# Gated linear attention feeding two MLP stages: a reordered opening, and squared terms kept in PSUM

## The chip, the cores and the metric

The kernel runs on one core of a Trainium2 chip. The metric is the device time of one execution in microseconds. Engines are named as the profile names them: PE (TensorE matmul), PEld (its weight load), DVE (VectorE), ACT (ScalarE), POOL (GpSimd) and SP (SyncE, which issues DMAs here). PSUM is the memory that PE writes; it has eight banks of 512 float32 per partition. SBUF holds everything else on the chip.

## The reference, cut to what matters

```python
# q, k, v, alpha: (4, 8, 768, 48)
for t in range(S):
    state = alpha[:, :, t, :, None] * state + einsum('bhd,bhe->bhde', k[:, :, t], v[:, :, t])
    y[:, :, t] = einsum('bhd,bhde->bhe', q[:, :, t], state)
x = y.transpose(0, 2, 1, 3).reshape(3072, 384)
p = domain_probs / domain_probs.sum(-1)             # (3072, 4)
x = sum(p[:, e:e+1] * (relu(x @ w1[e]) @ w2[e]) for e in range(4))   # 384 -> 1024 -> 384
h = x @ w_in                                        # 384 -> 2048
out = (h - tanh(h)) @ w_out                         # 2048 -> 384
```

## The kernel before

**Attention.** The sequence is cut into chunks of 128 steps, so there are 24 *units* (6 chunks of 4 batches), each with all 8 heads. For a unit `st_scan` (line 246) makes the decay products: a forward scan (250) into the first half of `fg`, a maximum and a reciprocal on four columns (255, 256), a small product `fc` (259) that carries the decay to the batch's next chunk, and a backward scan (261) into the second half. `st_prod` (265) multiplies q and k by them, `st_scores` (282) forms scores on PE, `st_kt` copies transposed keys, `st_mask` (301) masks scores, `st_out` (311) makes the output on PE, `st_upd` and `st_state` carry the state, `st_y` (353) copies the output to SBUF and `st_store` (359) sends it to DRAM. `st_flag` (271) takes a range check on ACT. `a_load`, `qk_load` and `v_load` bring a unit's inputs.

**MLP stages.** These run as *steps* `(g, block, f)`: g 0 to 3 are the four experts (8 steps a block), g 4 is the last MLP (16 steps a block). Tokens go in blocks of 512; g 0 begins with two blocks of 256. Every float32 operand is split in two parts, high and low, so a step has nine matmuls in `mm1` (line 479, into one PSUM tile `ph`) and nine in `mm2` (line 523, into three tiles `po`). Between them `evac1` (494) makes `hh` on ACT and `hl` on DVE; for g 4, `evac2` (503) calls `h_minus_tanh` (64): four ACT passes (`gu`, `gt` and two squares, both named `gs` in the trace), a mask `gmk` on POOL and five DVE passes (lines 71 to 75); `evac2_out` (514) then splits the result, `hh` on ACT and `hl` on POOL. `mm2` runs one to three steps behind `mm1` (`flush(depth)`), two in most of g 4.

Weights are split in `w_prep` (396): a cast on ACT (407) and a subtraction on POOL (408). The weights of g 4 come as 64-bit words and are converted during g 1 to 3.

**Order.** It is written by hand: the program order of each engine's instructions is the order of the calls (`manual_schedule`), and each engine runs its own queue in order. During g 0 the attention's stages are strung between the steps by `points` (372), four points to a unit and about two steps to a unit. Before the steps stands an opening (lines 562 to 656): loads, the first two units, the first 256 tokens' split (`x_parts`, 459), the normalisation of the probabilities (`p_norm`, 596), the splits of the first eight weights, and dummy matmuls (`busy`, 577). `at.tile(..., bufs=n)` gives n rotating buffers to a tag; a new use of a buffer waits for the last reader of its old contents.

Of the kernel before, what the change touches and what calls it, by code (L numbers as in the profile page):

```python
# [8 lines left out]
F32 = mybir.dt.float32  # L9
# [5 lines left out]
ALU = mybir.AluOpType  # L15
# [3 lines left out]
P = 128  # L19
# [18 lines left out]
def f32(ap):  # L38
    return ap.bitcast(F32)
# [138 lines left out]
def tile_kernel(ctx: ExitStack, tc: tile.TileContext, qka, a0, v, vT, pT, w12, w64, out):  # L178
# [43 lines left out]

    def a_load(u):
        c, b = divmod(u, B)
        t = at.tile([112, 513], F32, name="aa", tag="aa", bufs=2)
        nc.sync.dma_start(out=t, in_=qka[c, b, :, 1024:1537])
        unit[u]["aa"] = t

    def qk_load(u):
        c, b = divmod(u, B)  # L230
        t = at.tile([112, 1024], F32, name="qk", tag="qk", bufs=2)
        nc.sync.dma_start(out=t, in_=qka[c, b, :, 0:1024])
        unit[u]["qk"] = t

    def v_load(u):
        c, b = divmod(u, B)
        vt = at.tile([P, DM], F32, name="vraw", tag="vraw", bufs=4)
        nc.sync.dma_start(out=vt, in_=v[c, b])
        unit[u]["vt"] = vt
# [3 lines left out]
            return pso.tile(shape, F32, name=f"po{i}", tag=f"po{i}")  # L243
        return psa.tile(shape, F32, name="pa", tag="pa")

    def st_scan(u):
        s = unit[u]
        fg = at.tile([112, 1024], F32, name="fg", tag="fg", bufs=2)
        c_, r_ = fg[:, 0:512], fg[:, 512:1024]
        nc.vector.tensor_tensor_scan(out=c_, data0=s["aa"][:, 0:512], data1=c_beg, initial=0.0,  # L250
                                     op0=ALU.mult, op1=ALU.add)
        c127 = c_.rearrange("p (j t) -> p j t", t=C)[:, :, C - 1]

        den = at.tile([112, 4], F32, name="den", tag="den")
        nc.vector.tensor_scalar(out=den, in0=c127, scalar1=2.0 ** -62, scalar2=None, op0=ALU.max)
        nc.vector.reciprocal(out=r_end.rearrange("p (j t) -> p j t", t=C)[:, :, C - 1], in_=den)
        if u < NU - B:
            fc = at.tile([112, 4], F32, name="fc", tag="fc", bufs=4)
            nc.vector.tensor_tensor(out=fc, in0=c127, in1=a0s[:, u + B], op=ALU.mult)
            s["fc"] = fc  # L260
        nc.vector.tensor_tensor_scan(out=r_[:, ::-1], data0=s["aa"][:, 1:513][:, ::-1], data1=r_end[:, ::-1],  # L261
                                     initial=0.0, op0=ALU.mult, op1=ALU.add)
        s["fg"] = fg

    def st_prod(u):
        s = unit[u]
        prod = at.tile([112, 1024], F32, name="prod", tag="prod", bufs=3)
        nc.vector.tensor_tensor(out=prod, in0=s["qk"], in1=s["fg"], op=ALU.mult)  # L268
        s["prod"] = prod

    def st_flag(u):
        s = unit[u]
        ab = at.tile([112, 1024], BF16, name="ab", tag="ab")
        nc.scalar.activation(ab, s["fg"], AF.Abs, accum_out=flags[:, u:u + 1])

# [77 lines left out]
    def st_y(u):  # L353
        s = unit[u]
        s["y"] = at.tile([112, 512], F32, name="y", tag="y", bufs=2)
        for hf, r in halves():
            nc.scalar.copy(s["y"][r], s["py"][r])

    def st_store(u):
        s = unit[u]  # L360
        for hf, r in halves():
            nc.sync.dma_start(
                out=xr[u // 2].rearrange("(j r) t -> r j t", r=2 * D)[hf * D:(hf + 1) * D, :, (u % 2) * C:(u % 2 + 1) * C],
                in_=s["y"][r].rearrange("e (j t) -> e j t", t=C))

# [93 lines left out]
    def x_parts(t0, n, kb):  # L459
        t, raw = xt[0, t0], xraw[t0]  # L460
        nc.scalar.copy(t[:, 0, kb, :n], raw[:, kb, :n])
        nc.vector.tensor_tensor(out=t[:, 1, kb, :n], in0=raw[:, kb, :n], in1=f32(t[:, 0, kb, :n]), op=ALU.subtract)  # L462
        if kb == KB - 1:
            o = t0 % 512
            nc.sync.dma_start(out=xs[t0 // 512][:, :, :, o:o + n], in_=f32(t[:, :, :, :n]))

    def p_load(g, t0, n):
        t = sp.tile([P, 512], F32, name="pb", tag="pb")
# [10 lines left out]
    def mm1(st):  # L479
        g, bi, t0, n, f, _ = st  # L480
        w, x = slot[g * 8 + f], xt[g, t0]
        r = len(phs) % 5
        phs.append(0)
        if g == 4 and r >= 2:
            ph = late["p"].tile([P, 512], F32, name="ph", tag=f"po{r - 2}")
        else:
            ph = psh.tile([P, 512], F32, name="ph", tag="ph")
        seq = [(a, b, kb) for a, b in ((0, 0), (1, 0), (0, 1)) for kb in range(KB)]
        for m, (a, b, kb) in enumerate(seq):
            nc.tensor.matmul(ph[:, :n], w[:, a, 0, kb * P:(kb + 1) * P], x[:, b, kb, :n],  # L490
                             start=m == 0, stop=m == len(seq) - 1)
        return ph
# [10 lines left out]
    def evac2(st, ph):  # L503
        gp = late["g"]
        gg = h_minus_tanh(nc, ph, ca, gp.tile([P, 512], F32, name="gg", tag="gg"),
                          sp.tile([P, 512], F32, name="gu", tag="pb"),
                          gp.tile([P, 512], F32, name="gt", tag="gt"),
                          sp.tile([P, 768], F32, name="gs1", tag="wraw")[:, :512],
                          gp.tile([P, 512], F32, name="gs2", tag="gs2"),
                          gp.tile([P, 512], F32, name="ghu", tag="ghu"),  # L510
                          gp.tile([P, 512], I32, name="gmk", tag="gmk"))
        ggs[st] = gg
# [48 lines left out]
    with tc.manual_schedule():  # L561
        a_load(0)
        qk_load(0)
        a_load(1)
        v_load(0)
        nc.sync.dma_start(out=a0s, in_=a0)
        qk_load(1)
        v_load(1)
        pr = at.tile([P, NE, 24], F32, name="pr", tag="pr")
        nc.sync.dma_start(out=pr, in_=pT.rearrange("e (p j) -> p e j", p=P))  # L570
        w_load(0)
        w_load(1)

        wu = at.tile([P, 512], BF16, name="wu", tag="wu")
        nc.gpsimd.memset(wu, 0.0)
# [29 lines left out]
                                    op=ALU.mult)  # L605
            nc.sync.dma_start(out=pn.rearrange("e (p j) -> p e j", p=P), in_=pr)

        st_scan(0)
        st_prod(0)
        st_load(0)  # L610
        st_scores(0)
        st_kt(0)
        st_scan(1)
        st_mask(0)
        st_prod(1)
        w_load(2)
        w_load(3)
        st_out(0)
        st_scores(1)
        st_kt(1)  # L620
        st_load(1)
        st_y(0)
        st_store(0)
        st_flag(0)
        w_prep(0)
        st_mask(1)
        st_upd(0)
        busy(4)
        st_out(1)
        st_y(1)  # L630
        st_store(1)
        x_load(0, 0, 256)
        st_upd(1)
        st_state(0)
        st_state(1)
        st_flag(1)
        w_prep(1)
        busy(8)
        points(3)
        w_load(4)  # L640
        w_load(5)
        w_load(6)
        w_load(7)
        for kb in range(KB):
            x_parts(0, 256, kb)
        points(4)
        p_norm()
        w_prep(2)
        w_prep(3)
        w_load(8)  # L650
        w_load(9)
        p_load(0, 0, 256)
        w_prep(4)
        w_prep(5)
        w_prep(6)
        w_prep(7)

        conv = [(i, hf) for i in range(16) for hf in range(2)]

# [7 lines left out]
        for si, st in enumerate(steps):  # L667
# [141 lines left out]
```

## Time and profile before

| what | value |
|---|---|
| time, median of 3 runs | 1368.82 us (1367.76 to 1369.43) |
| profiled execution: time, span | 1368.58 us, 1366.7 us |
| busy: PE, PEld, DVE, ACT, POOL | 97%, 77%, 62%, 39%, 38% |
| chain that ended last: PE, DVE, issue | 73%, 21%, 3% |
| DMA | 118.60 MB, mean 87 GB/s |

The span runs from the first to the last instruction of the profiled execution. Busy shares are means over stages that differ: up to about 280 us attention and the first expert run together, from there to 922 us the other experts, and from there to the end the last MLP. A matmul's recorded end is modelled, so the distance between starts tells more than busy time.

### The profile page before, as it was taken

Reading aid. Unit: us, or ns where it says so; the run is one execution under the profiler, and the core shown is the slowest. Engines: PE = TensorE matmul, PEld = TensorE weight load, DVE = VectorE, ACT = ScalarE, POOL = GpSimd, SP = SyncE. Lnnn points to the kernel's source line nnn. Section 1 sums busy time; section 2 is a strip of 40 time slices with the busy share of each in tenths; the row PEclk is TensorE's granted clock in tenths of the full one; section 3 lists DMA queues with packets and bytes.
Section 4 is the critical chain, followed back from the end, with each engine's and each line's share of the span. In section 5 each row is a group of like instructions: output and inputs, shape, how many; then the busy total and the mean of one; then the engine's idle time right before and its main releaser. Section 6 shows DMA issues by size and latency. Waiting matters only on the chain.

```text
span 1366.7 us, 17887 instructions
## 1 busy us (share of the span) xinstructions
PE 1321.5 (97%) x6850; PEld 1057.5 (77%) x6850; DVE 847.8 (62%) x1213; ACT 527.9 (39%) x918; POOL 516.3 (38%) x403
## 2 busy tenths in 40 slices
PE   6699999999999999999999999998999999999996
PEld 4588888888888888888888888886777777777774
DVE  7777666622344344333345443328999999999996
ACT  4234323323111123111122111116666767676664
POOL 5211011004111125111133111127887877777774
PEclk8799999999999999999999999999999999999999
DMA  8456544343322224223334323241000000000000
GB/s 260 111 154 201 152 121 142 121 135 117 118 86 80 86 77 170 78 78 100 100 123 146 101 100 100 78 139 47 1 24 1 24 1 24 0 24 0 24 1 27
DMA packets 51457, 118.60 MB, mean 87 GB/s; under 512 B 5792, under 2 KB 28576, under 8 KB 48416
## 3 DMA queue, kind: packets, MB, share of 16 engines
q1 hardware_dynamic: 51360, 117.35, 26.8%
q8 instruction: 56, 0.92, 0.3%
q14 instruction: 41, 0.34, 0.1%
HBM read 92.12 MB, written 25.21 MB: 86 GB/s over the span
## 4 chain that ended last, share of the span: by engine, by line
PE 73%; DVE 21%; issue 3%; ACT 1%; DMA 1%; DVEq 0%; SPq 0%; ACTq 0%
PE po L536 34%; PE ph L490 33%; DVE ghu L73 6%; DVE gg L74 4%; DVE gg L75 3%; DVE ghu L71 2%; PE pa L292 2%; PE pa L325 1%; PE pa L328 1%; PE pa L317 1%; PE pa L287 1%; DVE am L306 1%; DVE prod L268 1%; DVE fg L250 1%; DVE fg L261 0%
## 5 line engine op out<-in xcount | busy, mean ns | idle before, releaser
L490 PE MATMUL ph<-xt,w 128*128 128x512 f32 (+1 forms) x2664 | 643.2, 386 | 0.4 <-DVE xt L462 0.4
L490 PEld LDWEIGHTS ph<-xt,w 128*128 128x128 f32 x2664 | 493.7, 189 | 104.1 <-issue 1.0
L536 PE MATMUL po<-hh,w 128*128 128x512 f32 (+1 forms) x1776 | 458.9, 393 | 15.6 <-ACT hh L518 8.1
L499 DVE SCALAR_TENSOR_TENSOR hl<-ph,hh 128x512 fp32r<-128x512 f32 (+1 forms) x200 | 133.8, 669 | 445.5 <-ACT hh L498 445.0
L536 PEld LDWEIGHTS po<-hh,w 128*128 128x128 f32 x1776 | 321.4, 188 | 112.4 <-ACT hh L518 34.2
L498 ACT ACTIVATE hh<-ph 128x512 fp32r<-128x512 f32 (+1 forms) x200 | 116.2, 581 | 594.0 <-PE ph L490 555.6
L536 PE MATMUL po<-hl,w 128*128 128x512 f32 (+1 forms) x888 | 247.9, 387 | 4.0 <-DVE hl L499 2.4
L536 PEld LDWEIGHTS po<-hl,w 128*128 128x128 f32 x888 | 160.1, 188 | 46.1 <-POOL hl L520 10.5
L70 POOL TENSOR_SCALAR gmk<-gu 128x512 int32<-128x512 f32 x96 | 176.0, 1833 | 25.6 <-ACT gu L66 25.2
L520 POOL TENSOR_TENSOR hl<-gg,hh 128x512 fp32r<-128x512 f32 x94 | 121.6, 1294 | 91.1 <-ACT hh L518 91.1
L73 DVE SCALAR_TENSOR_TENSOR ghu<-gs,ghu 128x512 f32<-128x512 f32 x96 | 132.3, 1379 | 0.0
L74 DVE SCALAR_TENSOR_TENSOR gg<-gs,ghu 128x512 f32<-128x512 f32 x96 | 97.4, 1015 | 12.7
L518 ACT CAST hh<-gg 128x512 fp32r<-128x512 f32 x96 | 59.7, 621 | 106.5 <-DVE gg L75 106.5
L552 POOL TENSOR_TENSOR acc<-acc,ptmp 128x512 f32<-128x512 f32 x51 | 64.6, 1298 | 83.7 <-DVE ptmp L548 83.7
L408 POOL TENSOR_TENSOR w<-wraw,w 128x768 fp32r<-128x768 f32 x26 | 48.7, 1872 | 122.8 <-issue 66.4
L349 POOL TENSOR_TENSOR state<-state,fc 112x192 f32<-112x192 f32 x20 | 11.9, 597 | 181.6 <-DVE state L340 145.1
L432 POOL TENSOR_TENSOR w<-wf,w 128x384 fp32r<-128x384 f32 x16 | 16.3, 1016 | 164.8 <-ACT w L431 164.8
L75 DVE COPY_PREDICATED gg<-gmk,ph 128x512 f32<-128x512 int32 x96 | 72.0, 750 | 9.9
L432 POOL TENSOR_TENSOR wo<-wf,wo 128x384 fp32r<-128x384 f32 x16 | 16.2, 1015 | 155.0 <-ACT wo L431 155.0
L66 ACT ACTIVATE gu<-ph 128x512 f32<-128x512 f32 x96 | 57.6, 600 | 34.8 <-PE ph L490 23.2
L68 ACT ACTIVATE gs<-gu,ca 128x512 f32<-128x512 f32 x96 | 69.7, 726 | 0.0
L69 ACT ACTIVATE gs<-gu,ca 128x512 f32<-128x512 f32 x96 | 69.4, 723 | 0.0
(91 smaller groups left out, 945.0 us busy)
## 6 DMA issues: line engine op xcount, KB each, us to landing
xt<-xs SPq DMA_DIRECT2D x18, 1536.0 KB, 7.1
r<-w SPq DMA_DIRECT2D x32, 384.0 KB, 4.2
qk<-qka SPq DMA_DIRECT2D x24, 448.0 KB, 4.5
wraw<-w SPq DMA_DIRECT2D x26, 384.0 KB, 3.1
xs<-xt SPq DMA_DIRECT2D x5, 1536.0 KB, 6.0
w64s<-wo SPq DMA_DIRECT2D x16, 384.0 KB, 3.0
w<-w64s SPq DMA_DIRECT2D x8, 768.0 KB, 4.3
pb<-pn SPq DMA_DIRECT2D x23, 256.0 KB, 4.3
```

The costliest lines, as they stand in the source:

```text
L68: nc.scalar.activation(s1, u, AF.Square, bias=ca[:, 0:1])
L69: nc.scalar.activation(s2, u, AF.Square, bias=ca[:, 1:2])
L70: nc.gpsimd.tensor_scalar(out=mk, in0=u, scalar1=T2, scalar2=None, op0=ALU.is_gt)
L73: nc.vector.scalar_tensor_tensor(out=hu, in0=s1, scalar=B1, in1=hu, op0=ALU.add, op1=ALU.mult)
L74: nc.vector.scalar_tensor_tensor(out=gg, in0=s2, scalar=B2, in1=hu, op0=ALU.add, op1=ALU.mult)
L75: nc.vector.copy_predicated(out=gg, mask=mk, data=ph)
L490: nc.tensor.matmul(ph[:, :n], w[:, a, 0, kb * P:(kb + 1) * P], x[:, b, kb, :n], start=m == 0, stop=m == len(seq) - 1)
L498: nc.scalar.activation(a[:, :n], ph[:, :n], AF.Relu)
L499: nc.vector.scalar_tensor_tensor(out=b[:, :n], in0=ph[:, :n], scalar=0.0, in1=f32(a[:, :n]), op0=ALU.max, op1=ALU.subtract)
L520: eng.tensor_tensor(out=b, in0=gg, in1=f32(a), op=ALU.subtract)
L536: nc.tensor.matmul(po[d][:, :n], w[:, wi, 1, d * P:(d + 1) * P], r[:, :n], start=f == 0 and pi == 0, stop=f == (7 if g < 4 else 15) and pi ...
L552: nc.gpsimd.tensor_tensor(out=a_, in0=a_, in1=tmp, op=ALU.add)
```

## The change

The input loads of four units and the first weights are put ahead, with three buffers for `aa` and `qk` in place of two. `st_scan` is cut in two (`st_c`, `st_r`); the second unit's forward scan stands ahead of the first unit's mask and its backward scan behind it. The `fc` product moves into `st_flag`. Stores of the attention's output are issued by ACT in place of SP; half of the output copy of units 0 and 1 goes to DVE. Weight splits 2 and 3 stand between the first points, and 4 to 7 behind steps 0 to 3; `p_norm` and the loads of weights 8 and 9 behind step 4. The store of the split x goes behind step 3 of its block (`x_keep`). In g 4 the tile `ph` has three places in turn in place of five, and the two banks set free hold `gs1` and `gs2`, one buffer each; before, these were in SBUF with two each.

```diff
-        t = at.tile([112, 513], F32, name="aa", tag="aa", bufs=2)
+        t = at.tile([112, 513], F32, name="aa", tag="aa", bufs=3)
-        t = at.tile([112, 1024], F32, name="qk", tag="qk", bufs=2)
+        t = at.tile([112, 1024], F32, name="qk", tag="qk", bufs=3)
...
     def st_flag(u):
         s = unit[u]
+        if u < NU - B:
+            s["fc"] = at.tile([112, 4], F32, name="fc", tag="fc", bufs=4)
+            nc.vector.tensor_tensor(out=s["fc"], in0=s["fg"].rearrange("p (j t) -> p j t", t=C)[:, 0:4, C - 1],
+                                    in1=a0s[:, u + B], op=ALU.mult)
...
         for hf, r in halves():
-            nc.scalar.copy(s["y"][r], s["py"][r])
+            if u < 2 and hf:
+                nc.vector.tensor_copy(s["y"][r], s["py"][r])
+            else:
+                nc.scalar.copy(s["y"][r], s["py"][r])
...
-            nc.sync.dma_start(
+            nc.scalar.dma_start(
                 out=xr[u // 2]...
...
-        r = len(phs) % 5
+        r = len(phs) % 3
         phs.append(0)
-        if g == 4 and r >= 2:
-            ph = late["p"].tile([P, 512], F32, name="ph", tag=f"po{r - 2}")
+        if g == 4 and r == 2:
+            ph = late["p"].tile([P, 512], F32, name="ph", tag="po0")
...
-                          sp.tile([P, 768], F32, name="gs1", tag="wraw")[:, :512],
-                          gp.tile([P, 512], F32, name="gs2", tag="gs2"),
+                          late["p"].tile([P, 512], F32, name="gs1", tag="po1"),
+                          late["p"].tile([P, 512], F32, name="gs2", tag="po2"),
...
-        st_scan(0)
+        st_c(0)
+        st_r(0)
         st_prod(0)
-        st_load(0)
+        st_c(1)
+        w_prep(0)
         st_scores(0)
         st_kt(0)
-        st_scan(1)
         st_mask(0)
+        busy(4)
+        st_r(1)
         st_prod(1)
...
-        busy(8)
-        points(3)
...
+        busy(10)
+        points(2)
+        st_flag(1)
+        w_prep(2)
         for kb in range(KB):
             x_parts(0, 256, kb)
+        points(3)
+        w_prep(3)
         points(4)
-        p_norm()
-        w_prep(2)
-        w_prep(3)
-        w_load(8)
-        w_load(9)
-        p_load(0, 0, 256)
-        w_prep(4)
-        w_prep(5)
-        w_prep(6)
-        w_prep(7)
+        st_state(0)
+        st_state(1)
...
+                if f == 3:
+                    x_keep(t0, n)
+                if bi == 0 and f < 4:
+                    w_prep(4 + f)
+                if bi == 0 and f == 4:
+                    w_load(8)
+                    w_load(9)
+                    p_norm()
+                    p_load(0, 0, 256)
```

DVE's queue from the second unit's product to the first step's `hl` and the scan behind it. In the kernel before (`am` is the masked score tile, `sm` and `pr` belong to `p_norm`, `xt` is the split x):

```order
L306 TENSOR_TENSOR am<-pa,mask 128x512 x2
...
L268 TENSOR_TENSOR prod<-qk,fg 112x1024
L462 TENSOR_TENSOR xt<-xraw,xt 128x256 x3
L599 TENSOR_TENSOR sm<-pr 128x24
L601 TENSOR_TENSOR sm<-sm,pr 128x24 x2
L602 TENSOR_SCALAR sm<-sm 128x24
L603 RECIPROCAL sm<-sm 128x24
L604 TENSOR_TENSOR pr<-pr,sm 128x96
L499 SCALAR_TENSOR_TENSOR hl<-ph,hh 128x256
L306 TENSOR_TENSOR am<-pa,mask 128x512 x2
L250 SCALAR_TENSOR_TENSOR fg<-aa,c_beg 112x512
```

In the changed kernel:

```order
L364 COPY y<-pa 48x512
...
L270 TENSOR_TENSOR prod<-qk,fg 112x1024
L277 TENSOR_TENSOR fc<-fg,a0s 112x4
L471 TENSOR_TENSOR xt<-xraw,xt 128x256 x3
L277 TENSOR_TENSOR fc<-fg,a0s 112x4
L509 SCALAR_TENSOR_TENSOR hl<-ph,hh 128x256
L312 TENSOR_TENSOR am<-pa,mask 128x512 x2
L250 SCALAR_TENSOR_TENSOR fg<-aa,c_beg 112x512
```

The six instructions of `p_norm` no longer stand between the split x and the first `hl`; they come after step 4.

ACT's queue from the split of x on. In the kernel before (`w` casts are weight splits, `ab` the range check):

```order
L461 CAST xt<-xraw 128x256 x3
L407 CAST w<-acc_88 128x768 x2
L407 CAST w<-acc_89 128x768 x2
L407 CAST w<-acc_90 128x768 x2
L498 ACTIVATE hh<-ph 128x256
L299 COPY kt<-pa 128x448
L498 ACTIVATE hh<-ph 128x256
```

In the changed kernel:

```order
L366 COPY y<-pa 48x512
L371 DMA xr_91<-y 48x4x128 x2
L280 ACTIVATE ab,flags<-fg 112x1024 x2
L416 CAST w<-acc_88 128x768
L470 CAST xt<-xraw 128x256 x3
L280 ACTIVATE ab,flags<-fg 112x1024
L416 CAST w<-acc_88 128x768
L508 ACTIVATE hh<-ph 128x256
L305 COPY kt<-pa 128x448
L416 CAST w<-acc_89 128x768
L508 ACTIVATE hh<-ph 128x256
```

One weight cast is left between the split x and the first `hh` where six stood, and the others follow one to a step; two store issues and two range checks now stand ahead of the third weight's cast.

## Rows read from the trace of the kernel before

**Rows 1.** Windows: busy us (instructions) per engine, PE clock, DMA share, GB/s.
```profile
20.00:40.00 20.00, 9.01 (x49) 7.19 (x47) 18.84 (x17) 10.16 (x18) 18.84 (x14) 0.66 0.61 192
...
922.00:1345.00 423.00, 413.78 (x1700) 309.41 (x1699) 397.73 (x471) 288.94 (x502) 320.56 (x205) 1.00 0.04 14
```

**Rows 2.** Chain that ended last, the opening: start us, us, what.
```profile
25.95 4.51 DVE xt L462 x3
30.46 1.75 DVE sm L599
...
39.36 0.42 DVE hl L499
...
40.98 1.14 DVE fg L250
...
43.82 1.24 DVE prod L268
...
48.18 2.23 PE ph L490 x9
```

**Rows 3.** Timeline, to 80 us: start us, us, engine, line, operation.
```profile
19.10 1.81 POOL L408 TENSOR_TENSOR w<-wraw,w 128x768 fp32r<-128x768 f32 x1 [14.61 <-ACT w L407]
19.30 2.69 DVE L250 TENSOR_TENSOR_SCAN fg<-aa,c_beg 112x512 f32<-112x512 f32 x1
...
28.18 11.04 POOL L408 TENSOR_TENSOR w<-acc,w 128x768 fp32r<-128x768 f32 x6
...
64.83 0.93 SPq L362 DMA_DIRECT2D xr<-y  x2
...
77.15 1.09 DVE L462 TENSOR_TENSOR xt<-xraw,xt 128x256 fp32r<-128x256 f32 x3
```

**Rows 4.** Timeline of DVE inside a block of g 4.
```profile
1045.60 0.68 DVE L71 SCALAR_TENSOR_TENSOR ghu<-ph,gu 128x512 f32<-128x512 f32 x1
...
1046.79 1.50 DVE L73 SCALAR_TENSOR_TENSOR ghu<-gs,ghu 128x512 f32<-128x512 f32 x1
1048.42 0.88 DVE L74 SCALAR_TENSOR_TENSOR gg<-gs,ghu 128x512 f32<-128x512 f32 x1
...
1050.05 0.67 DVE L71 SCALAR_TENSOR_TENSOR ghu<-ph,gu 128x512 f32<-128x512 f32 x1
```

**Rows 5.** Timeline of DVE at the first step of g 4.
```profile
926.54 0.68 DVE L73 SCALAR_TENSOR_TENSOR ghu<-gs,ghu 128x512 f32<-128x512 f32 x1
927.33 0.69 DVE L74 SCALAR_TENSOR_TENSOR gg<-gs,ghu 128x512 f32<-128x512 f32 x1
...
928.75 1.89 DVE L548 TENSOR_TENSOR ptmp<-po,pb 128x512 f32<-128x512 f32 x3
```

**Rows 6.** Timeline of POOL in g 4.
```profile
929.21 1.49 POOL L70 TENSOR_SCALAR gmk<-gu 128x512 int32<-128x512 f32 x1 [2.74 <-ACT gu L66]
...
1046.44 1.30 POOL L520 TENSOR_TENSOR hl<-gg,hh 128x512 fp32r<-128x512 f32 x1 [1.25 <-ACT hh L518]
1047.71 1.94 POOL L70 TENSOR_SCALAR gmk<-gu 128x512 int32<-128x512 f32 x1
```

**Rows 7.** Groups by line, 1007.11 to 1290.86 us: count, busy us, mean ns.
```profile
L68 ACT ACTIVATE gs<-gu,ca 128x512 f32<-128x512 f32 x64 | 46.5, 726 | 0.0
```

**Rows 8.** Chain that ended last, steps of g 1 and of g 4.
```profile
442.67 2.04 PE po L536 x9
...
1007.11 2.87 PE po L536 x9
...
1023.05 2.10 PE ph L490 x9
...
1078.06 2.87 PE po L536 x9
...
1355.96 3.05 PE po L536 x12
```

**Rows 9.** Timeline of PE, the first step of g 4.
```profile
921.91 2.27 PE L490 MATMUL ph<-xt,w 128*128 128x512 f32 x9
```

More of the change, by code (lines that the diff above doesn't have):

```diff
@@ L244, in bank, with st_c, st_r, st_scan @@
         return psa.tile(shape, F32, name="pa", tag="pa")
-    def st_scan(u):
+    def st_c(u):
         s = unit[u]
-        fg = at.tile([112, 1024], F32, name="fg", tag="fg", bufs=2)
-        c_, r_ = fg[:, 0:512], fg[:, 512:1024]
+        s["fg"] = at.tile([112, 1024], F32, name="fg", tag="fg", bufs=2)
+        c_ = s["fg"][:, 0:512]
         nc.vector.tensor_tensor_scan(out=c_, data0=s["aa"][:, 0:512], data1=c_beg, initial=0.0,
                                      op0=ALU.mult, op1=ALU.add)
-        c127 = c_.rearrange("p (j t) -> p j t", t=C)[:, :, C - 1]
         den = at.tile([112, 4], F32, name="den", tag="den")
-        nc.vector.tensor_scalar(out=den, in0=c127, scalar1=2.0 ** -62, scalar2=None, op0=ALU.max)
+        nc.vector.tensor_scalar(out=den, in0=c_.rearrange("p (j t) -> p j t", t=C)[:, :, C - 1], scalar1=2.0 ** -62,
+                                scalar2=None, op0=ALU.max)
         nc.vector.reciprocal(out=r_end.rearrange("p (j t) -> p j t", t=C)[:, :, C - 1], in_=den)
[L257 to L263, printed above, removed]
+    def st_r(u):
+        s = unit[u]
+        nc.vector.tensor_tensor_scan(out=s["fg"][:, 512:1024][:, ::-1], data0=s["aa"][:, 1:513][:, ::-1],
+                                     data1=r_end[:, ::-1], initial=0.0, op0=ALU.mult, op1=ALU.add)
+    def st_scan(u):
+        st_c(u)
+        st_r(u)
     def st_prod(u):
@@ L462, in x_parts, with x_keep @@
         nc.vector.tensor_tensor(out=t[:, 1, kb, :n], in0=raw[:, kb, :n], in1=f32(t[:, 0, kb, :n]), op=ALU.subtract)
-        if kb == KB - 1:
-            o = t0 % 512
-            nc.sync.dma_start(out=xs[t0 // 512][:, :, :, o:o + n], in_=f32(t[:, :, :, :n]))
+    def x_keep(t0, n):
+        o = t0 % 512
+        nc.sync.dma_start(out=xs[t0 // 512][:, :, :, o:o + n], in_=f32(xt[0, t0][:, :, :, :n]))
     def p_load(g, t0, n):
@@ L563, in tile_kernel @@
         qk_load(0)
+        nc.sync.dma_start(out=a0s, in_=a0)
         a_load(1)
         v_load(0)
-        nc.sync.dma_start(out=a0s, in_=a0)
         qk_load(1)
+        w_load(0)
         v_load(1)
+        w_load(1)
+        a_load(2)
+        qk_load(2)
+        w_load(2)
+        v_load(2)
+        w_load(3)
+        a_load(3)
+        qk_load(3)
+        v_load(3)
         pr = at.tile([P, NE, 24], F32, name="pr", tag="pr")
         nc.sync.dma_start(out=pr, in_=pT.rearrange("e (p j) -> p e j", p=P))
-        w_load(0)
-        w_load(1)
+        w_load(4)
         wu = at.tile([P, 512], BF16, name="wu", tag="wu")
@@ L606, in p_norm @@
             nc.sync.dma_start(out=pn.rearrange("e (p j) -> p e j", p=P), in_=pr)
-        st_scan(0)
+        st_c(0)
+        st_r(0)
         st_prod(0)
-        st_load(0)
+        st_c(1)
+        w_prep(0)
         st_scores(0)
         st_kt(0)
-        st_scan(1)
         st_mask(0)
+        busy(4)
+        st_r(1)
         st_prod(1)
-        w_load(2)
-        w_load(3)
         st_out(0)
+        st_y(0)
+        st_store(0)
         st_scores(1)
         st_kt(1)
[L621 to L625, printed above, removed]
         st_mask(1)
-        st_upd(0)
+        w_prep(1)
         busy(4)
@@ L632, in tile_kernel @@
         x_load(0, 0, 256)
[L633 to L637, printed above, removed]
-        busy(8)
-        points(3)
-        w_load(4)
         w_load(5)
@@ L643, in tile_kernel @@
         w_load(7)
+        st_upd(0)
+        st_upd(1)
+        st_flag(0)
+        busy(10)
+        points(2)
+        st_flag(1)
+        w_prep(2)
         for kb in range(KB):
             x_parts(0, 256, kb)
+        points(3)
+        w_prep(3)
         points(4)
-        p_norm()
-        w_prep(2)
-        w_prep(3)
-        w_load(8)
-        w_load(9)
-        p_load(0, 0, 256)
-        w_prep(4)
-        w_prep(5)
-        w_prep(6)
-        w_prep(7)
+        st_state(0)
+        st_state(1)
         conv = [(i, hf) for i in range(16) for hf in range(2)]
@@ L706, in tile_kernel @@
             flush(depth)
+            if g == 0 and last and f == 3:
+                x_keep(t0, n)
             if g == 0 and not last:
@@ L716, in tile_kernel @@
                         x_parts(*nxt[1:], kb)
+                if f == 3:
+                    x_keep(t0, n)
+                if bi == 0 and f < 4:
[5 more added lines that the diff above has]
+                    p_load(0, 0, 256)
             if g == 1 and bi == 0 and f == 2:
```

## The prediction

> **What bounds the kernel now.** I read the windows by stage first, then the chain of waits in each stage, then the timeline of the engine that the chain runs on. In the last MLP (g 4, from 922 us) DVE is busy 397.73 of 423 us while PE has small gaps; in the middle stages no other engine comes near that, and PE sets the pace: nine matmuls follow nine at 2.04 us on the chain [rows 1, 8]. Between 20 and 40 us PE is busy 9.01 of 20 us at a mean granted clock of 0.66, with DVE and POOL both at 18.84 [rows 1]. So two stretches have something to give: g 4, bound by DVE, and the opening, bound by a chain of waits. The stretch between them is left as it is.
>
> **Why DVE bounds g 4.** One step's five passes start at 1045.60 and the next step's at 1050.05: 4.45 us a step [rows 4]. L73 takes 1.50 us there and L74 0.88. At the first step, before POOL has anything to subtract, the same two take 0.68 and 0.69 [rows 5]. Both read two SBUF tensors (`gs` and `ghu`). L71 in the block, which reads `ph` from PSUM and `gu` from SBUF, takes 0.68 [rows 4], and the three L548 at 928.75 (one PSUM operand) take 1.89 together although POOL's L70 starts at 929.21 [rows 5, 6]. That L70 takes 1.49, the one beside L74 1.94 [rows 6]. So a DVE pass with two SBUF operands and POOL get in each other's way; a pass with one operand in PSUM does not.
>
> **The change in g 4.** L73 and L74 keep their count (96 each), but `gs` comes from PSUM. I price them by the first step: L73 to L74 0.79, L74 with L75 928.75 - 927.33 = 1.42, L71 with L72 1046.79 - 1045.60 = 1.19; together 3.40 us a step [rows 4, 5]. POOL needs 1.49 + 1.30 = 2.79 [rows 6]; in the three steps of a block that also split the next block's x there is a third subtraction of about 1.30, so 4.09. ACT is busy 288.94 us over some 95 steps, 3.04 a step [rows 1]. What is late next is PE. Where PE runs freely in g 4 nine matmuls take 2.10 us (not the 2.04 of g 1), so a step takes 4.20 [rows 8]: DVE has 0.8 us to spare, ACT 1.1, POOL 1.4, or 0.1 in the splitting steps.
>
> The added waits: with one `gs1` and one `gs2`, ACT's two squares of step i+1 wait for L73 and L74 of step i. Behind them on ACT stands the cast `hh` of step i, and for that wait POOL's `hl` and PE's `mm2`. ACT's four passes at 0.73 and L74 end about 4 us after `mm1` of step i; the first square of step i+1 starts 4.20 and two passes, 5.7 us, after it. So the wait is over before it is asked for as long as PE sets the pace; if the cover went, it would cost one pass, 0.8 us, a step. With three `ph` in place of five, `mm1` of step i+3 waits for L75 of step i, three steps or 12.6 us after its own `mm1` began; `mm1`, ACT's four passes, L74 and L75 take 2.10 + 2.9 + 1.42 = 6.4 of these. I take nothing for both.
>
> The trace has no ACT pass that writes PSUM. From the SBUF form of 0.726 us [rows 7] I take no change; from below a square could be as short as the shortest DVE pass (0.68), from above as long as POOL's longest on 512 elements (1.94). The first is nothing to the sum; the second is a rival below.
>
> Sum for g 4: it runs from 921.91 to 1355.96 + 3.05 = 1359.01, 437.1 us [rows 8, 9]. PE has 96 `mm1`, 96 `mm2` and the last `mm2` of g 3 to do, 193 x 2.10 = 405.3. I keep the five block changes at what they cost now over 2.10 (2.87 - 2.10 = 0.77 each, 3.9) [rows 8] and allow 1 us for the splitting steps: 410.2, that is 26.9 us less. Four middle blocks give 1078.06 - 1007.11 = 70.95 less 68.0 each, about 12 together; the rest is the first block, where POOL's extra work stalls PE more, and the end, where PE waits out DVE's backlog. At 2.04 a group the gain would be 193 x 0.06 = 11.6 more, 38.5; with no relief for DVE it is 0.
>
> **The change in the opening.** Before, the split of x runs from 25.95 to 30.46 (4.51 us; the same three take 1.09 at 77.15, with POOL free) [rows 2, 3]. Behind it on DVE stands `p_norm`, slowed from 30.46 on by six weight splits on POOL (11.04 us from 28.18), so that the first `hl` comes at 39.36, unit 3's product at 43.82 and the third step's `mm1` at 48.18 [rows 2, 3]. Afterwards `hl` stands right behind the split.
>
> - *Up to the split of x.* `fc` out of the scan, the second forward scan before the mask, half of two output copies on DVE: each should take a microsecond or less off the first two units (an estimate: all are single passes). But the second range check, the third weight's cast and two store issues (0.93 us a pair on SP [rows 3]) now stand on ACT's queue ahead of x, and x waits for both stores to land. I take 0, between 2 us earlier and 2 later.
> - *From there to the first `hl`.* Unit 2's product ends by 25.95, where the split begins. On the chain, from the end of a product (43.82 + 1.24 = 45.06) to the end of the next `mm1` (48.18 + 2.23 = 50.41) PE takes 5.35 at its low clock; `hh` follows with about the 0.4 of `hl`. So `hl` at 25.95 + 5.35 + 0.4 = 31.7 in place of 39.36: 7.6 us earlier [rows 2].
> - *The four splits moved into steps 0 to 3.* Each is a cast on ACT and a subtraction on POOL. A scan beside one took 2.69 in place of 1.14, 1.55 more [rows 2, 3]. Those behind steps 0 and 2 come on POOL just when a scan is due; those behind 1 and 3 wait on ACT behind a range check, which waits for the backward scan, and miss it. Two collisions: 3.1 us later.
> - *`p_norm` behind step 4.* It then lies beside PE's scores and `mm1` (5.35 us at the low clock), and no split runs: nothing. Without that cover it costs up to the 8.9 us it takes now (30.46 to 39.36).
> - *Loads ahead, stores on ACT, `x_keep`.* ACT has room for 0.93 a unit in g 0: nothing, since PE is not held by loads there. If ACT did become late by it, 22 units would cost at most 20 us.
>
> The Trainium skill, "SBUF — State Buffer", section "Who interferes with whom", says that the pair of ports which VectorE and GpSimd share is a lock held for a whole instruction, and that who issues first decides who blocks. The 1.55 above agrees: POOL began 0.20 us before the scan. By the rule alone a split that begins after a scan costs the scan nothing, so the four splits would cost between 0 and 6.2; it speaks against spreading them between scans rather than for it.
>
> Opening: 7.6 - 3.1 = 4.5 us less, between 10 less and 7 more (all four splits collide, part of `p_norm` uncovered, x late).
>
> **Sum.** The profiled execution took 1368.58 us, 1.9 outside its span of 1366.7; the median of the runs is 1368.82, so it stands for them. 1368.6 - 26.9 - 4.5 = 1337.2; I say 1337.
>
> **Rivals.**
> 1. *PE also regains 2.04 a group, and the opening its full 7.6.* For it: DVE and POOL would be less busy. Against: in the freest stretches of g 4 it is 2.10 with the clock granted in full. 1368.6 - 38.5 - 4.5 = 1326, or 1322 with the opening.
> 2. *The opening gives nothing.* The splits collide at every scan, ACT's longer queue holds x. For it: all of these run beside scans that already are on the chain. 1341.7 with no gain, 1349 with 7 lost.
> 3. *DVE stays close to the bound.* One of L73 and L74 is not relieved, or the single buffers and the splitting steps stall PE now and then. With one relieved, DVE's step is 4.45 - 0.84 = 3.6 or 4.45 - 0.2 = 4.25; with half of g 4's gain lost, 1351.
> 4. *The change doesn't relieve DVE at all.* POOL still holds up passes that read PSUM and one SBUF tensor: 1364. Rows 4 and 5 speak against it.
> 5. *Slower: ACT's squares are slow into PSUM.* Place: L68 and L69, 192 passes. ACT's other work is 3.04 - 1.45 = 1.59 a step; ACT is the bound above 4.20, and the kernel is slower than before once the step exceeds (437.1 + 4.5 + 2.7)/96 = 4.63, which is 1.52 us a square, twice what it takes now. At POOL's 1.94 the step is 5.47 and the time 1368.6 - 4.5 + 96 x 5.47 - 437.1 = 1452. No pass of ACT on 512 elements is near this.
>
> **How the numbers follow.** Forecast (1330 to 1344) 0.57; first rival 0.10; second 0.17; third 0.08; fourth 0.04; fifth 0.04. A measurement of this kernel tells a change of about 0.2%, 2.7 us, from none. Faster: all but the fifth and half of the fourth, 0.94; same 0.02; slower 0.04. The range of 1327 to 1350 takes in the second rival and the edge of the first; outside lie some two in ten.
>
> **What would show it.** Right in g 4: L73 and L74 near 0.7, L70 near 1.5, a step of 4.20 between starts on PE, DVE under 85% busy, and PE on the chain there. Wrong: a wait of L68 or L69 on DVE in every step, ACT's squares longer than 0.75, `mm1` waiting for L75, or L73 still above 1. Right in the opening: the first `hl` near 32 us and the third step's `mm1` near 42; wrong: a scan of over 2 us in every unit up to step 4, or x landing after 28 us.

## The result and the profile after

The changed kernel takes 1334.06 us (median of 4 runs, 1333.15 to 1335.29) against 1368.52 for the kernel before on the same chip (median of 4): ratio 0.9749, 95% interval [0.9732, 0.9765]. The forecast was 1337. The profiled execution took 1333.86, 1.9 outside its span of 1332.0. The total hides two errors of the forecast that largely cancel: g 4 gave 8 us more than was said, and the opening, which was to give 4.5 us, gave nothing. That the total came within 3 us of the forecast is in part luck.

Windows by stage of the changed kernel, columns as in [rows 1], the second one ending before the last step:

```profile
20.00:40.00 20.00, 10.76 (x63) 8.46 (x59) 15.57 (x23) 8.33 (x16) 8.84 (x9) 0.73 0.68 178
922.00:1320.00 398.00, 398.00 (x1728) 324.17 (x1727) 319.23 (x482) 285.29 (x510) 286.09 (x208) 1.00 0.04 16
```

In g 4 PE is busy without a gap, and DVE went from 94% to 80%. In the opening DVE and POOL are much less busy than before, and yet PE gained only 1.75 us of work in 20 us: they had not been the whole of its wait.

DVE's timeline inside a block of g 4, to be read against [rows 4], and the groups of the page for POOL's L70 and ACT's L68 over all of g 4 (count | busy us, mean ns | idle before and its releaser):

```profile
1003.86 0.69 DVE L71 SCALAR_TENSOR_TENSOR ghu<-ph,gu 128x512 f32<-128x512 f32 x1
...
1005.07 0.68 DVE L73 SCALAR_TENSOR_TENSOR ghu<-gs,ghu 128x512 f32<-128x512 f32 x1
1005.88 0.69 DVE L74 SCALAR_TENSOR_TENSOR gg<-gs,ghu 128x512 f32<-128x512 f32 x1
...
1008.06 0.69 DVE L71 SCALAR_TENSOR_TENSOR ghu<-ph,gu 128x512 f32<-128x512 f32 x1 [0.62 <-ACT gt L67]
```

```profile
L70 POOL TENSOR_SCALAR gmk<-gu 128x512 int32<-128x512 f32 x96 | 143.2, 1491 | 69.1 <-ACT gu L66 69.1
...
L68 ACT ACTIVATE gs<-gu,ca 128x512 f32<-128x512 f32 x96 | 67.0, 698 | 0.2 <-DVE ghu L73 0.2
```

L73 has 0.68 where it had 1.50, L74 0.69 for 0.88, and POOL's L70 1.49 for 1.94 [rows 4, 6]; as means over all 96 steps L73 went from 1.38 to 0.68, L74 from 1.02 to 0.69 and L70 from 1.83 to 1.49. DVE's step is 1008.06 - 1003.86 = 4.20 and now begins with a wait for ACT, so DVE is no longer the bound. The single buffers cost nothing: ACT waited 0.2 us for them in 96 steps, as the prediction had worked out, and a square into PSUM takes 0.698, less than the 0.726 into SBUF [rows 7].

The chain of waits of the changed kernel, g 4:

```profile
998.37 2.18 PE po L546 x9
...
1008.95 2.10 PE ph L500 x9
...
1029.90 2.04 PE ph L500 x9
...
1322.71 3.03 PE po L546 x12
```

PE is nearly the whole chain now. A block's first `mm2` takes 2.18 in place of 2.87 [rows 8]. And within one block there are two speeds, 2.10 and 2.04 a group; before, the chain had 2.04 only outside g 4. PE's first group of g 4, against [rows 9]:

```profile
923.57 2.27 PE L500 MATMUL ph<-xt,w 128*128 128x512 f32 x9
```

So g 4 runs from 923.57 to 1325.74, 402.2 us against 437.1: 34.9 less, which is the whole gain of the kernel. It starts 1.66 us later than before; up to there the changed opening has lost rather than won. (Three experiments below have the old opening and start g 4 at 922.06, 919.83 and 919.33; two more have the new one and start it at 922.99 and 924.07. Executions of one opening differ by up to 2.7 us, so the 1.66 shows the sign of the loss and not its size.)

The opening's chain, against [rows 2]:

```profile
34.81 0.42 DVE hl L509
...
36.43 2.56 DVE fg L250
...
45.05 2.23 PE ph L500 x9
...
65.39 0.11 DVE sm L618
...
66.79 1.88 DMA pn<-pr
...
70.54 7.25 DMA xraw<-xr
```

The first `hl` comes 4.55 us earlier than before and the third step's `mm1` 3.13. Both are gone again by the second block, whose x is loaded at 70.54. The timeline of the first 37 us shows who holds whom:

```profile
10.48 1.81 POOL L417 TENSOR_TENSOR w<-wraw,w 128x768 fp32r<-128x768 f32 x1 [6.00 <-ACT w L416]
10.88 2.49 DVE L260 TENSOR_TENSOR_SCAN fg<-aa,r_end 112x512 f32<-112x512 f32 x1
12.98 2.72 ACTq L371 DMA_DIRECT2D xr<-y  x2
14.69 0.60 PE L293 MATMUL pa<-ident,prod 112*128 112x112 f32 x4 [2.36 <-DVE prod L270]
15.74 0.53 ACT L305 COPY kt<-pa 128x448 f32<-128x448 f32 x1 [2.79 <-DVE y L364]
16.90 1.29 DVE L312 TENSOR_TENSOR am<-pa,mask 128x512 f32<-128x512 f32 x2 [1.55 <-PE pa L298]
17.08 1.81 POOL L417 TENSOR_TENSOR w<-wraw,w 128x768 fp32r<-128x768 f32 x1 [4.79 <-ACT w L416]
20.94 0.69 DVE L364 COPY y<-pa 48x512 f32<-48x512 f32 x1 [2.75 <-ACT y L366]
25.09 1.23 DVE L260 TENSOR_TENSOR_SCAN fg<-aa,r_end 112x512 f32<-112x512 f32 x1
25.16 2.75 POOL L417 TENSOR_TENSOR w<-acc,w 128x768 fp32r<-128x768 f32 x1 [6.27 <-ACT w L416]
26.35 2.65 DVE L270 TENSOR_TENSOR prod<-qk,fg 112x1024 f32<-112x1024 f32 x1
26.94 1.02 ACT L470 CAST xt<-xraw 128x256 fp32r<-128x256 f32 x3 [1.86 <-DMA xraw<-xr]
29.15 0.98 PE L293 MATMUL pa<-ident,prod 112*128 112x112 f32 x4 [6.61 <-DVE fc L277]
29.82 1.93 POOL L417 TENSOR_TENSOR w<-acc,w 128x768 fp32r<-128x768 f32 x1 [1.90 <-DVE xt L471]
30.00 1.76 DVE L277 TENSOR_TENSOR fc<-fg,a0s 112x4 f32<-112x4 f32 x1
36.07 1.83 POOL L417 TENSOR_TENSOR w<-acc,w 128x768 fp32r<-128x768 f32 x1 [1.70 <-issue]
36.35 2.63 DVE L250 TENSOR_TENSOR_SCAN fg<-aa,c_beg 112x512 f32<-112x512 f32 x1
```

Four of the five weight splits on POOL in this stretch catch a DVE pass with two SBUF operands. The fifth, at 17.08, stands beside `am`, which reads PSUM and one SBUF tile, and neither gets longer (in the kernel before the pair at 16.59, with POOL idle, took 1.29 too). The split at 10.48 ends at 12.29; the scan issued at 10.88 ends at 13.37, 1.08 later, as if it had begun when POOL was done. The `fc` of four elements a partition is the purest case: issued at 30.00, 0.18 after a split, it lasts 1.76 and ends at 31.76, with the split (31.75). It goes the other way too: the split at 25.16 began 0.07 after a scan and took 2.75 for 1.81, which is why `prod`, issued at 26.35, ended only at 29.00. The Trainium skill, "SBUF — State Buffer", section "Who interferes with whom", has a DVE instruction with two SBUF inputs contend with a GpSimd one that reads SBUF, and an exclusive lock where one of them waits for the whole instruction; these rows agree to 0.01 us for `fc`.

The other loss is on ACT: the two stores that it now issues stand in its queue from 12.98 to 15.70, since the second of them waits for the half of `y` that DVE copies at 14.66, behind `prod`. Behind them stands `kt`, which starts at 15.74. For the second unit, DVE's half of `y` waits 2.75 until ACT's half is done: the halves ran one after the other. PE's mean granted clock from 16 to 20 us is 0.61 after its idle 2.36; before, it was at 1.00 there.

### The profile page after: what moved, and what is told of

Read it like the earlier page. It is cut to its first block, busy times and chain, and to the rows that moved or that the text cites. A ratio compares the mean times of both kernels' runs of the same rounds, so it can differ in the third digit from the quotient of the medians.

```text
span 1332.0 us, 17950 instructions
## 1 busy us (share of the span) xinstructions
PE 1303.1 (98%) x6856; PEld 1071.3 (80%) x6856; DVE 759.0 (57%) x1215; ACT 518.0 (39%) x916; POOL 474.8 (36%) x403
## 4 chain that ended last, share of the span: by engine, by line
PE 92%; DVE 3%; issue 1%; DMA 1%; ACT 1%; SPq 0%; ACTq 0%; DVEq 0%
PE po L546 44%; PE ph L500 44%; PE pa L298 2%; PE pa L331 1%; PE pa L334 1%; DVE fg L250 1%; DMA xraw<-xr 1%; DVE prod L270 1%; PE pa L323 0%; PE pa L293 0%; DVE am L312 0%; DVE fg L260 0%; DVE hl L509 0%; DVE acc L555 0%; DVE xt L471 0%
## 5 line engine op out<-in xcount | busy, mean ns | idle before, releaser
L546 PE MATMUL po<-hh,w 128*128 128x512 f32 (+1 forms) x1776 | 449.4, 388 | 0.0
L546 PEld LDWEIGHTS po<-hh,w 128*128 128x128 f32 x1776 | 327.3, 189 | 72.5 <-issue 3.5
L546 PEld LDWEIGHTS po<-hl,w 128*128 128x128 f32 x888 | 165.2, 189 | 35.6 <-DVE hl L530 1.8
L70 POOL TENSOR_SCALAR gmk<-gu 128x512 int32<-128x512 f32 x96 | 143.2, 1491 | 69.1 <-ACT gu L66 69.1
L71 DVE SCALAR_TENSOR_TENSOR ghu<-ph,gu 128x512 f32<-128x512 f32 x96 | 66.3, 691 | 53.9 <-ACT gt L67 53.1
L75 DVE COPY_PREDICATED gg<-gmk,ph 128x512 f32<-128x512 int32 x96 | 72.0, 750 | 12.0 <-POOL hl L530 2.7
L74 DVE SCALAR_TENSOR_TENSOR gg<-gs,ghu 128x512 f32<-128x512 f32 x96 | 66.5, 692 | 12.7
L68 ACT ACTIVATE gs<-gu,ca 128x512 f32<-128x512 f32 x96 | 67.0, 698 | 0.2 <-DVE ghu L73 0.2
L69 ACT ACTIVATE gs<-gu,ca 128x512 f32<-128x512 f32 x96 | 66.9, 697 | 0.1
L72 DVE TENSOR_TENSOR ph<-ph,gt 128x512 f32<-128x512 f32 x96 | 66.2, 690 | 0.0
```

The source lines that it names most:

```text
L68: nc.scalar.activation(s1, u, AF.Square, bias=ca[:, 0:1])
L69: nc.scalar.activation(s2, u, AF.Square, bias=ca[:, 1:2])
L70: nc.gpsimd.tensor_scalar(out=mk, in0=u, scalar1=T2, scalar2=None, op0=ALU.is_gt)
L71: nc.vector.scalar_tensor_tensor(out=hu, in0=ph, scalar=C4, in1=u, op0=ALU.mult, op1=ALU.mult)
L72: nc.vector.tensor_tensor(out=ph, in0=ph, in1=th, op=ALU.subtract)
L74: nc.vector.scalar_tensor_tensor(out=gg, in0=s2, scalar=B2, in1=hu, op0=ALU.add, op1=ALU.mult)
```

## The experiments

Two theories of the sum: (A) all of the gain is the PSUM operands, through the lock between DVE and POOL, and the opening's reorder is a small loss; (B) the opening gives part, or the relief in g 4 comes from the buffers and the three `ph`. Each ratio is to runs of the kernel before on the same chip.

**psum_only.** The kernel before with the change in g 4 alone.

```diff
-        r = len(phs) % 5
+        r = len(phs) % 3
...
-                          sp.tile([P, 768], F32, name="gs1", tag="wraw")[:, :512],
+                          late["p"].tile([P, 512], F32, name="gs1", tag="po1"),
...
```

> The kernel before with the g 4 part of the change alone: gs1 and gs2 in PSUM, three ph. Theory: L73 and L74 read one SBUF operand only and no longer get in POOL's way, and the whole gain of the change is here; in the changed kernel g 4 ran from 923.57 to 1325.74 us, 402.2 in place of 437.1, and began 1.7 us later than before, so this kernel should take 1368.5 - 34.9 - 1.4 (its end after the last matmul was shorter by that) = 1332, a little under the changed kernel's 1334. Rival (opening and g 4 share the gain, as the prediction had it, 4.5 and 26.9): 1341.

**opening_only.** The changed kernel with these lines as before: the opening alone.

```diff
-        r = len(phs) % 3
+        r = len(phs) % 5
...
-                          late["p"].tile([P, 512], F32, name="gs1", tag="po1"),
+                          sp.tile([P, 768], F32, name="gs1", tag="wraw")[:, :512],
...
```

> The changed kernel with the g 4 part undone: gs in SBUF with two buffers, five ph. Theory: the opening as changed brings nothing, it starts g 4 about 1.7 us later: 1370, between 1368 and 1372, and the first expert's third mm1 near 45 us as in the changed kernel. Rival (the prediction's 4.5 us less): 1364.

psum_only took 1331.62 us (5 runs), ratio 0.9745 [0.9731, 0.9758]; opening_only 1370.74 (5 runs), ratio 1.0036 [1.0022, 1.0051]. So the part in g 4 makes all of the gain, and the opening alone makes the kernel slower by about 5 us, more than the 1.7 that was expected. In opening_only the third step's `mm1` starts at 43.3, some 5 us earlier than before, and the first 512-wide `mm1` at 116.12 against 114.94 (112.36 to 115.08 in the three experiments with the old opening): what was won by 43 us is lost by 116. The two ratios multiply to 0.978, 0.3% above the changed kernel's 0.9749; that is about the width of the intervals. Against 0.9745 for the part in g 4 alone, the opening costs half a microsecond in the changed kernel, and alone it costs five. No run shows a gain by it; how much it loses stays open.

**sbuf_single.** The kernel before with one `gs1` and one `gs2`, still in SBUF, and `ph` in three places: the new waits without the relief.

```diff
-        r = len(phs) % 5
+        r = len(phs) % 3
...
-                          sp.tile([P, 768], F32, name="gs1", tag="wraw")[:, :512],
-                          gp.tile([P, 512], F32, name="gs2", tag="gs2"),
+                          gp.tile([P, 512], F32, name="gs1", tag="gs1", bufs=1),
+                          gp.tile([P, 512], F32, name="gs2", tag="gs2", bufs=1),
```

> The kernel before with gs1 and gs2 in SBUF with one buffer each, and three ph in place of five. Theory (port, not buffers): L73 stays at 1.50 us, a step at 4.45, time 1368 within 3. Rival (the number of buffers or ph places is what moved g 4): near 1333. Second rival (single buffers stall ACT and are paid for in the changed kernel too): over 1372, with L68 or L69 waiting for DVE in every step.

It took 1369.6 us in one run, 0.7 above the slowest of the nine runs of the kernel before beside it (1364.99 to 1368.88). Two groups of its page:

```profile
L73 DVE SCALAR_TENSOR_TENSOR ghu<-gs,ghu 128x512 f32<-128x512 f32 x96 | 132.2, 1377 | 0.0
L68 ACT ACTIVATE gs<-gu,ca 128x512 f32<-128x512 f32 x96 | 69.7, 726 | 52.4 <-DVE ghu L73 51.8
```

L73 stays slow, so neither the buffers nor the places of `ph` bring the gain. With DVE as the bound, ACT does wait for the single buffer, 51.8 us in 96 steps, and inside the blocks it costs nothing, because DVE is later anyway: from one block's first `mm2` to the next it is 71.0 us, and 70.9 in the kernel before. With PE as the bound the wait is 0.2.

**ghu_psum.** The kernel before with `gs` still in SBUF; `ghu`, which DVE writes itself, takes the two banks, and `ph` has three places: ACT writes nothing to PSUM.

```diff
-        r = len(phs) % 5
+        r = len(phs) % 3
...
-                          gp.tile([P, 512], F32, name="ghu", tag="ghu"),
+                          late["p"].tile([P, 512], F32, name="ghu", tag=f"po{1 + len(phs) % 2}"),
```

> The kernel before with gs in SBUF as before, but ghu, which L71 and L73 write and L73 and L74 read, in the two PSUM banks, two buffers; three ph. Theory: one PSUM operand is enough whichever it is, so L73 and L74 take 0.7 us, L70 1.5, time 1332 to 1335. Rival (the gain comes from ACT writing its squares into PSUM): no gain, L73 at 1.5, 1368.

It took 1330.75 us in one run.

```profile
L73 DVE SCALAR_TENSOR_TENSOR ghu<-gs,ghu 128x512 f32<-128x512 f32 x96 | 65.8, 685 | 0.0
L68 ACT ACTIVATE gs<-gu,ca 128x512 f32<-128x512 f32 x96 | 69.8, 727 | 0.0
```

Either operand in PSUM relieves the pass. ACT's square into SBUF keeps its 0.727, so the 0.03 that it saves into PSUM plays no part.

**p_norm_early.** The changed kernel with `p_norm` and its load ahead of the steps.

```diff
         w_prep(3)
+        p_norm()
+        p_load(0, 0, 256)
         points(4)
...
-                    p_norm()
-                    p_load(0, 0, 256)
```

> The changed kernel with p_norm, its store and the load of the first probabilities moved back from behind step 4 to the place behind the third weight's split, ahead of the steps. Theory: behind step 4 it held up the state copy and with it a PSUM tile that PE waited 1.25 us for, and on SP's queue the loads and the second block's x (landed at 77.8 us); ahead of the steps DVE is idle some 3 us. Block 1's first mm1 2 to 4 us earlier than at 81.5, time 1330 to 1332. Rival (PE was bound by the scan chain there anyway): 1334.

**splits_apart.** The changed kernel with the weight splits moved away from scans, in pairs.

```diff
         st_c(1)
-        w_prep(0)
...
+        w_prep(0)
         st_mask(1)
         w_prep(1)
+        w_prep(2)
...
-                if bi == 0 and f < 4:
-                    w_prep(4 + f)
+                if bi == 0 and f in (1, 3):
+                    w_prep(3 + f)
+                    w_prep(4 + f)
```

> The changed kernel with weight splits moved off the scans: 0, 1 and 2 behind the second unit's key copy, 4 and 5 together behind step 1, 6 and 7 behind step 3. Theory: four passes of DVE waited for a split (the backward scan of unit 1, unit 2's product, the forward scans of units 3 and 4), each 1.3 to 1.4 us on the chain, so up to 5.4 us less, with all scans at 1.2 us; 1329 to 1331. Rival (x's landing and PE's low clock set the pace): under 2 us, 1333.

**opening_mended.** Both of these, and the whole of `y` copied by ACT again.

```diff
-            if u < 2 and hf:
-                nc.vector.tensor_copy(s["y"][r], s["py"][r])
-            else:
-                nc.scalar.copy(s["y"][r], s["py"][r])
+            nc.scalar.copy(s["y"][r], s["py"][r])
```

> The changed kernel with both edits (p_norm early, splits apart) and the whole output copy of units 0 and 1 on ACT. Theory: the gains add, 5 to 8 us, 1326 to 1329, faster than both kernels and than the kernel with g 4's part alone (0.9745 of before). Rival (the same chain bounds all): 1331 to 1334.

p_norm_early took 1331.13 us, ratio 0.9739 [0.9724, 0.9754]; splits_apart 1327.03, 0.9703 [0.9688, 0.9718]; opening_mended 1323.97, 0.9682 [0.9668, 0.9695]. The changed kernel has 0.9749. What moving `p_norm` brings alone lies inside the intervals, though its trace shows the second block's load issued at 67.11 in place of 70.54. Moving the splits brings 0.5%, clear of the intervals, and all three together bring 0.7%, about 9 us; both are faster than was expected (1329 to 1331 and 1326 to 1329). The edits of `p_norm` and of `y` are not told apart in the third. Against psum_only, which has the same g 4 behind the old opening, opening_mended is 0.6% faster, about 8.6 us: an opening that gives more than the forecast's 4.5.

In the timeline of splits_apart these passes have no split beside them:

```profile
11.30 1.22 DVE L260 TENSOR_TENSOR_SCAN fg<-aa,r_end 112x512 f32<-112x512 f32 x1
24.64 1.22 DVE L270 TENSOR_TENSOR prod<-qk,fg 112x1024 f32<-112x1024 f32 x1
33.06 1.22 DVE L250 TENSOR_TENSOR_SCAN fg<-aa,c_beg 112x512 f32<-112x512 f32 x1
```

The 2.49, 2.65 and 2.63 of the changed kernel are 1.22 here. Its stores still sit long on ACT. In opening_mended, with both halves of `y` on ACT, the first pair is issued in 0.92, x lands at 25.59 and the steps follow:

```profile
12.85 0.92 ACTq L368 DMA_DIRECT2D xr<-y  x2
25.59 1.02 ACT L467 CAST xt<-xraw 128x256 fp32r<-128x256 f32 x3 [3.44 <-DMA xraw<-xr]
30.97 0.42 DVE L506 SCALAR_TENSOR_TENSOR hl<-ph,hh 128x256 fp32r<-128x256 f32 x1 [2.40 <-ACT hh L505]
39.73 2.29 PE L497 MATMUL ph<-xt,w 128*128 128x256 f32 x9
```

These are the times that the prediction gave for the opening, with the splits in other places: the first `hl` near 31, the third step before 42.

**weights_turned.** For the two speeds of PE in g 4: the changed kernel with the weights of each block of g 4 taken in an order turned by 8 steps. Either the speed goes with the step of the block, or with the weights.

```diff
-        w, x = slot[g * 8 + f], xt[g, t0]
+        w, x = slot[g * 8 + (f if g < 4 else (f + 8) % 16)], xt[g, t0]
...
-        w = slot[g * 8 + f]
+        w = slot[g * 8 + (f if g < 4 else (f + 8) % 16)]
```

> The changed kernel, with g 4's hidden blocks taken in another order: steps 0 to 7 use the weights 8 to 15 and steps 8 to 15 the weights 0 to 7 (the sum over them is the same). In the changed kernel nine matmuls take 2.10 us in the first ten steps of every block of g 4 and 2.04 in the last six. Theory: it goes with the weights' place, since weights 0 to 7 lie in tiles of their own and 8 to 15 in the rotating slots of the earlier stages; then the first eight steps run at 2.04 and the slow groups come from step 8 on. Rival: it goes with the time since the block's start (x just written, stores going out): the first ten steps stay at 2.10. Time 1334 in both.

It took 1334.01 us in one run. The chain of its block from 998.74, in which the same places stand as above (f 5 at 1009.06, f 10 at 1029.65):

```profile
998.74 2.17 PE po L546 x9
...
1009.06 2.04 PE ph L500 x9
...
1029.65 2.10 PE ph L500 x9
```

The fast and the slow half have changed places: the speed goes with the weights. The groups on the weights 0 to 7 take 2.08 to 2.11, nearly all on 8 to 15 take 2.04 to 2.06. The exceptions stand between groups on the slow weights: where `mm1` and `mm2` take their weights from different halves, a group on the fast ones can take 2.09 too. In the program's layout the tiles of 8 to 15, those of g 0 to 3 as well, start 256 bytes past a multiple of 512 in a partition of SBUF; the tiles of 0 to 7 lie behind a tile of 4 bytes, and start at 384 past one.

**weights_at_256.** opening_mended with that small tile lengthened, so that the tiles of 0 to 7 start like the others.

```diff
-                rs = late["w"].tile([112, 1], F32, name="rs", tag="rs")
+                rs = late["w"].tile([112, 97], F32, name="rs", tag="rs")[:, 0:1]
```

> The mended opening, with the 4-byte tile rs of L735's pool made 388 bytes, so that the eight weight tiles of f 0 to 7 of g 4 start 384 bytes later, at 256 bytes past a multiple of 512, where the tiles of f 8 to 15 start; as it stands, they start at 384 bytes past one. In the runs so far the groups with the weights of f 0 to 7 take 2.09 to 2.10 us in g 4 and those of f 8 to 15 take 2.04, whatever the place of the step in the block. If the place of the start within 512 bytes is what does it, all groups of g 4 but those at a block's bounds take 2.04, and the kernel takes 6 blocks x 17 groups x 0.055 = 5.6 us less than the mended opening: 1318.4, ratio to before 0.964. Rival: it is the region of SBUF, or that these tiles were written by ACT and POOL and not by a DMA: then the groups stay at 2.09 to 2.10 and the time at 1324, ratio 0.968.

**weights_at_512.** The same with less: a start at a multiple of 512.

```diff
-                rs = late["w"].tile([112, 97], F32, name="rs", tag="rs")[:, 0:1]
+                rs = late["w"].tile([112, 33], F32, name="rs", tag="rs")[:, 0:1]
```

> As the run before it, but moved by 128 bytes, so that the tiles of f 0 to 7 start at a multiple of 512. If the start must lie at a multiple of 256 bytes, the groups take 2.04 here too and the kernel 1318.4 us. If they must lie where those of f 8 to 15 do, at 256 past a multiple of 512, the groups with the weights of f 0 to 7 stay at 2.09 to 2.10 and the time at 1324.

weights_at_256 took 1318.34 us (5 runs), ratio 0.9637 [0.9624, 0.965], and weights_at_512 1319.09 in one run. The chain of opening_mended, f 7 and f 10 of a block, then the same two of weights_at_256:

```profile
1007.96 2.10 PE ph L497 x9
...
1020.49 2.04 PE ph L497 x9
```

```profile
1005.99 2.04 PE ph L497 x9
...
1018.23 2.04 PE ph L497 x9
```

Every group in the inside of a block takes 2.04, with either start. The kernel takes 5.6 us less, as the expectation had it (6.2 by the ratios, since the two ran on different chips), and g 4 in the traces 396.6 in place of 401.9. The longer tile also moves what lies behind the weights, `ptmp` and the tiles of g 4, while PE's other operands (`xt`, `hh`, `hl`) keep their places; and the turned order had shown that the speed goes with the weights, so it is their start that does it. Why a weight tile 128 bytes off a multiple of 256 slows matmuls by 3% isn't shown: the traces give the weight loads a mean of 188 ns at either speed. Other offsets weren't tried. weights_at_256, at 0.9637 of the kernel before where the changed kernel has 0.9749, is the fastest version here.

## Why the prediction was right, and where it was not

**G 4, the mechanism: right.** A pass of L73's or L74's kind with one operand in PSUM does not get in POOL's way; L73, L74 and L70 came out at the forecast's 0.7 and 1.5, the step at 4.20, DVE at 80%. psum_only shows that the gain is here, sbuf_single that it isn't the buffers, ghu_psum that it isn't ACT.

**G 4, the size: 34.9 in place of 26.9.** Three terms were mis-sized. (1) "193 x 2.10": the 191 groups from 923.57 to 1319.85 have a mean of 2.075 with the block changes in it, because half of the weights run at 2.04: about 5 us less. That is a part of the first rival, whose reason against ("in the freest stretches of g 4 it is 2.10") was read from groups on the slow weights alone. (2) "I keep the five block changes at what they cost now": they cost 0.08 over 2.10, not 0.77, so 3.5 less; PE had waited there for ACT's copy of `po`, which stood behind a cast that waited for DVE's L75. (3) The 1 us for the splitting steps didn't arise: POOL's third subtraction is relieved as well (mean 1.30 in place of 1.77). Against it stands the end, where the last two groups take 1325.74 - 1319.85 = 5.9 in place of 4.2. -5.2 - 3.5 - 1.0 + 1.7 = -8.0. Behind the last matmul there are 6.3 us where there were 7.7, 1.4 less. That goes with the opening and not with g 4: the traces with the old opening have 7.7 to 8.4 us there, psum_only among them, and those with a changed one 5.7 to 6.4. Why isn't shown.

**The opening: wrong by some 6 us, 1.66 lost in the profiled pair for 4.5 won.** The step that failed is "Up to the split of x: I take 0", with the sentence behind it that unit 2's product ends by 25.95.
- The product ended at 29.00, because the split of weight 2 and a scan had met before it. From a product's end to `hl` the prediction took 5.35 + 0.4; 29.00 + 5.75 = 34.75, and `hl` came at 34.81. The interval was right, its beginning 3.05 us off.
- Two more things stood in that step: the scan of unit 1 beside the split of weight 0 (1.27 longer), and ACT held by its store. splits_apart and opening_mended take them away one after the other. The cited rule had been read as saying that a split which begins after a scan costs nothing; the split itself then ends later and catches the next pass, here the product, which took 2.65 in place of 1.22.
- "Two collisions: 3.1 us": the two scans behind steps 0 and 2 took 2.63 and 2.56 in place of 1.22, 2.75 us together; this term held. (Its 1.55 a collision set 2.69, an instruction's whole time, against 1.14, the chain's part of one; by whole times it is 2.69 - 1.22 = 1.47.) But the term counted only the splits that had been moved behind steps.
- "`p_norm` behind step 4: nothing": it isn't hidden. Its arithmetic, 1.4 us from 65.39, and its store stand on the chain of waits, and so does what comes behind them. This is the stretch from 65 us in the changed kernel:

```profile
66.79 0.40 SPq L625 DMA_DIRECT2D pn<-pr  x1
67.01 0.71 DVE L348 COPY state<-pa 48x192 f32<-48x192 f32 x2
67.78 2.08 PE L298 MATMUL pa<-prod 48*128 48x128 f32 x14 [1.25 <-DVE state L348]
70.54 0.39 SPq L465 DMA_DIRECT2D xraw<-xr  x1
77.82 1.02 ACT L470 CAST xt<-xraw 128x256 fp32r<-128x256 f32 x3 [4.90 <-DMA xraw<-xr]
```

The copy of the state stood behind `p_norm` on DVE, PE waited 1.25 for it, and its granted clock was 0.50, the lower level, from 68 to 72 us (0.64 before). On SP's queue the loads of the next block came behind the store of `pn` and its load back. The sixth step's `mm1` is still 0.49 us ahead of the kernel before, the seventh's, behind this stretch, 0.92 late: 1.4 us. Moving `p_norm` alone shows no more than the intervals are wide, so this is the smaller part.

**The rivals.** The second, the opening gives nothing, was right in its place and reason (splits at scans, ACT's queue), beside a larger g 4. The third to the fifth are excluded by the rows above. The first was right in part: the groups on half of the weights run at 2.04. -34.9 + 1.66 - 1.4 give -34.6; the profiled executions differ by 1368.58 - 1333.86 = 34.7.

## What to carry to other kernels

A DVE pass with two SBUF operands and a POOL instruction that reads SBUF beside it pay for each other: where POOL works all the time, put one of the operands in PSUM; where it works now and then, put its work where DVE has no such pass. Two SBUF operands are not the only such case: in the kernel before, `p_norm`'s L602, with one SBUF operand and a constant, took 1.73 us beside the splits, and the same pass 0.18 in the changed kernel. When work is moved to a free engine or another queue, check what stands behind it there, and start a forecast's chain at the end of the last piece of work that can be late, not at the time it had before. When one matmul group has two durations in a trace, sort them by operand before taking either as the rate.

## What was not expected of the hardware

- The start of a weight tile within SBUF sets the pace of matmuls: 2.10 us for nine at 384 bytes past a multiple of 512, 2.04 at 0 or 256, at the full granted clock; 5.6 us of this kernel.
- ACT's square takes 0.698 us into PSUM and 0.726 into SBUF.
- A DMA issue on ACT whose data another engine still writes holds ACT's later work (2.72 us for a pair that takes 0.92 at 64.30, where both halves are ready).
